# Gated linear attention and SwiGLU: the way down of five blocks by 15 products of 128 columns instead of 7 products of 192

## The chip, the cores and the metric

The kernel runs on one core of a Trainium2 chip. The metric is the device time of one execution in microseconds (us). TensorE (PE) multiplies matrices, VectorE (DVE), ScalarE (ACT) and GpSimd (POOL) work elementwise, SyncE (SP) issues transfers. The instructions of an engine stand in an order that the program fixes, and wait on semaphores for what the other engines have to deliver.

## What is computed

Two stages, all in fp32. The attention runs over 4 batches, 8 heads, 768 positions and 48 features; its output, seen as 3072 tokens of 384 features, is the input of a SwiGLU layer with 1536 hidden features:

```python
f = 1.0 / (1.0 + np.exp(-f_logit))
for t in range(S):
    state = f[:, :, t, :, None] * state + np.einsum('bhd,bhe->bhde', k[:, :, t], v[:, :, t])
    y[:, :, t] = np.einsum('bhd,bhde->bhe', q[:, :, t], state)
x = y.transpose(0, 2, 1, 3).reshape(B * S, H * D)
g = x @ w_gate
return (g * (1.0 / (1.0 + np.exp(-g))) * (x @ w_val)) @ w_out
```

## The kernel before

**Blocks.** The tokens are cut into six blocks, one for each chunk of 128 positions (c = 0 to 5); a block holds 128 positions of 4 batches, 512 tokens. While block c goes through the SwiGLU layer, the attention of chunk c + 1 is worked out between its products. Block 0 is a plain layer (`mlp_plain`: products of 512 columns at L939, then `downs_abreast`: products of 384 columns at L962, whose four results are copied out by ScalarE and VectorE in turn at L983).

**Way up of blocks 1 to 5** (`mlp_fifteen`). Gate and val come from a scheme that multiplies a 3x3 arrangement of weight parts by a 3x2 arrangement of token parts with 15 products in place of 18. The table `PRODUCTS` names for each product r the bank that it is added to (A, B, c or o), the weight part or weight sum, and the token part or token sum (t1 to t15, made by VectorE). There are four such sets of 15 products (`triple(j)`), each product of 256 columns (L1155). Between the products ScalarE copies banks out, VectorE adds, ScalarE applies silu (L1171) and VectorE multiplies by val (L1107); the products of the last two steps finish late (`finish_late`). The hidden activations `h` lie in six parts, by the feature third and the token half.

**Way down of blocks 1 to 5** (`down_seven`). The output of 512 tokens by 384 features is made by a scheme with 7 products in place of 8: each product multiplies one of four parts of `h` (or one of the hidden sums that VectorE makes, 128x768 elements each: `hs` and sums in place of parts of `h`, L1056 and L1059) by half of the columns of `w_out` (or a sum of weights, `ws1`, `ws2`, `ws4`). A product is 12 matmuls of 192 columns by 128 rows; a matmul in fp32 is two instructions, so a block has 168 of them (L1258, the last product L1321). The sums of weights are made once, in block 1, by four multiplications by -1 on ScalarE (L1094) and four accumulating DMAs of 576 KB, which GpSimd's queue issues (L1095).

**What sets the order.** The order is written out by hand. `in_turn_of_time` walks through the products, adds up their planned costs (`PRODUCT`, `DOWN`), and emits a piece of attention when its planned time has come (`SCORES` for the score products, `CHAINS` for the elementwise steps of a chunk and batch, `times`). `lag` puts an operation behind the next product. `in_order` then fixes the order of the instructions on each engine.

**Attention of one batch in a chunk**, as its lines stand: sigmoid by ScalarE (L670, with a table load ahead of it), a transposition on VectorE into `gates` (L681), one of k into `qT` (L692), a running product `tails` (a scan, L702), its reciprocal (L705), `kT` (L648), a transposition for the queue (L722), a second scan (L736), a transposition of q (L740), `qT` (L648), the state (L900) and the decayed state (L654). TensorE uses them in `y` (L836, L847, L872), `dS` (L818) and the scores `sc` (L761, L767), which VectorE masks (L800, L802). The result returns through ScalarE (yT, L854) and ten small DMAs at a time on GpSimd's queue (xT<-yT, L861).

**PSUM.** Banks A (2), B (1), o (2, which c shares) and three for attention.

Of the kernel before, what the change touches and what calls it, by code (L numbers as in the profile page):

```python
# [9 lines left out]
FP32 = mybir.dt.float32  # L10
# [4 lines left out]
ALU = mybir.AluOpType  # L15
# [275 lines left out]
def short_path(ctx, tc, ident, least, judge, q, k, v, f_logit, moe_w_gate, moe_w_val, moe_w_out, out):  # L291
# [633 lines left out]

    def hidden_tile(h, j):


        if j % 2 not in h:
            h[j % 2] = ffn.tile([128, NP // 2, 4, TH], FP32, tag="h", name="h", bufs=2)  # L930
        return h[j % 2][:, j // 2]
# [39 lines left out]
    def downs_abreast(c, h):  # L971
# [3 lines left out]
        def step(n):  # L975
# [3 lines left out]
            for b in range(B):  # L979
                down_part(banks[b], c, h, b, n)  # L980
                if n == NF - 1:
                    ob = rooms_of[b // 2][:, b % 2, :]
                    (nc.vector.tensor_copy if b % 2 else nc.scalar.copy)(ob, banks[b])  # L983
                    nc.gpsimd.dma_start(out=out[b * S + c * C:b * S + (c + 1) * C, :], in_=ob)
# [13 lines left out]
    PRODUCT, DOWN, PLAIN, PLAIN_DOWN = 0.86, 3.9, 2.57, 2.65  # L998
# [10 lines left out]
    whole = NJ * TRIPLE + 7 * DOWN  # L1009
    between = [n * TRIPLE - 0.05 for n in range(NJ)]  # L1010
    inside = [t - PRODUCT for t in between]
    down = [NJ * TRIPLE + n * DOWN / 2 - 0.05 for n in range(14)]
    SCORES = {c: scores for c, scores in zip(range(2, NCH), (
        ((12, "b"), (between[2], "o"), (down[2], "A"), (down[5], "A")),
        ((PRODUCT - 0.05, "b"), (between[1], "o"), (inside[3], "o"), (down[3], "A")),
        *[((down[10] - whole, "A"), (inside[1], "o"), (inside[3], "o"), (down[3], "A"))] * (NCH - 4)))}
    CHAINS = {c: chains for c, chains in zip(range(2, NCH), (
        (chain(2.6, 4.8, 8.6), chain(14.5, 21.7, 23.2, 21.2, 19.6), chain(30, 37, 43.6), chain(57.4, 56.6, 61)),
        (chain(-12, -8.5, -5), chain(3.5, 6, 9), chain(16, 28, 33, 21.5, 23.5), chain(40.1, 53, 55, 44.5, 52)),
        *[(chain(-19.4, -11.2, -9.5), (-7.5, -6.3, 1.3, 2.2, 3.2, 5.5, 8, 10), chain(16, 28, 33, 21.5, 23.5), chain(40.1, 53, 55, 44.5, 52))] * (NCH - 4)))}  # L1020
    LAST = 72.5
    APART = {1: (1, 3), 2: (1, 2), **{c: (2,) for c in range(3, NCH - 1)}, NCH - 1: range(1, NJ)}

    def times(c):
        at = [t for t, _ in SCORES[c]]
        outputs = [*at[1:], down[10] if c + 1 in SCORES and SCORES[c + 1][0][0] < -1 else LAST]
        sigmoid = [-14 if c == 3 else SCORES[c - 1][-1][0] - whole - 0.01 if c > 3 else 0, -1.5 if c == 3 else at[0] - 0.01, *[t - 0.01 for t in at[1:]]]
        masks = {"b": 2, "o": 0.9, "A": 1.5}
# [3 lines left out]
    def score_bank(u):  # L1032
# [4 lines left out]
        return {"o": banks_o, "A": banks_a}[kind].tile([128, 512], FP32, tag=kind, name="sc")  # L1037
# [14 lines left out]
    DOWN_SUMS_AT = (13, 13.01, 26.2, 26.21, 34.5, 34.51, 43, 43.01)  # L1052
# [30 lines left out]
    down_sums = {}  # L1083

    def down_weight_sums():

        DH = DM // 2
        b11, b12 = w_out[:, 0:NP, 0:DH], w_out[:, 0:NP, DH:DM]
        b21, b22 = w_out[:, NP:NF, 0:DH], w_out[:, NP:NF, DH:DM]
        for i in (1, 2, 4):  # L1090
            down_sums[i] = comb.tile([128, NP, DH], FP32, tag=f"ws{i}", name=f"ws{i}")
# [441 lines left out]
```

## Time and profile before

| | |
|---|---|
| median of 3 runs | 589.19 us (588.88 to 590.15) |
| profiled execution | 588.79 us, of which the profile's span is 587.1 us |
| granted TensorE clock | 0.997 |
| PE / DVE / ACT / POOL busy | 576.2 / 472.1 / 306.4 / 116.5 us |
| way down of block 1 | 194.89 to 230.89 us, with attention between its products |
| way down of block 3 | 379.95 to 414.53 us |
| way down of block 5 | from 553.65 us, no attention; last matmul ends at about 582 us |

The profiled execution is 0.4 us below the median; 1.7 us of its time lie outside the span. Times below are microseconds from the start of the span. In a row of the timeline stand the start, the duration from the first start to the last end, the engine, the line, the operation, what it writes and reads, shape and count; consecutive instructions of one kind are one row. A matmul's row contains the time in which its last columns leave the array, so the pace of matmuls is read from the starts of two rows and not from their durations.

### The profile page before, as it was taken

The numbers are of one execution on the slowest core, as the hardware profiler recorded it, in microseconds if no ns is written. First come the engines' busy times: TensorE is split into PE (matmuls) and PEld (weight loads), VectorE is DVE, ScalarE is ACT, GpSimd is POOL, SyncE is SP. The second block draws the span as 40 slices with busy tenths as digits, with TensorE's granted clock in tenths as the row PEclk, the third lists the DMA queues.
The fourth block names the chain that finished last, engine by engine and source line by source line (L and its number), as shares of the span: only waits on it lengthen the run. The fifth ranks groups of instructions, "written<-read, shape, count | busy, mean of one in ns | idle before, by whom it ended". The sixth has DMA issues, their size and how long they took to land.

```text
span 587.1 us, 12325 instructions
## 1 busy us (share of the span) xinstructions
PE 576.2 (98%) x4644; PEld 476.8 (81%) x4644; DVE 472.1 (80%) x828; ACT 306.4 (52%) x589; POOL 116.5 (20%) x253
## 2 busy tenths in 40 slices
PE   7899999999999999999999999999999999999996
PEld 5744445667888999888999888899988899988996
DVE  7978898999989977998985988994978971766641
ACT  2587778023887422677640576732486830366600
POOL 4140344311132241021130030330030330000000
PEclk9999999999999999999999999999999999999998
DMA  9999696433769576462444532444331100100001
GB/s 190 267 284 271 206 231 155 91 106 107 138 145 132 110 164 154 117 118 72 106 107 114 136 88 65 105 110 112 95 101 29 35 13 3 55 1 2 0 1 56
DMA packets 118785, 64.48 MB, mean 110 GB/s; under 512 B 76592, under 2 KB 109168, under 8 KB 118720
## 3 DMA queue, kind: packets, MB, share of 16 engines
q1 hardware_dynamic: 106448, 48.49, 34.0%
q0 software_dynamic: 11120, 13.58, 10.2%
q10 hardware_dynamic: 1152, 1.57, 0.7%
q8 instruction: 37, 0.61, 0.5%
q14 instruction: 28, 0.23, 0.1%
HBM read 49.64 MB, written 8.65 MB: 99 GB/s over the span
## 4 chain that ended last, share of the span: by engine, by line
PE 94%; ACT 2%; DVE 2%; DMA 1%; issue 1%; ACTq 0%; DVEq 0%
PE o L1258 20%; PE A L1155 17%; PE B L1155 14%; PE c L1155 6%; PE o L962 5%; PE o L1155 5%; PE gate L939 5%; PE val L939 5%; PE o L1321 3%; PE y L872 2%; PE dS L818 2%; PE y L836 2%; PE sc L761 2%; PE y L847 2%; DMA fraw<-in_f_logit_dram 1%; PE sc L767 1%
## 5 line engine op out<-in xcount | busy, mean ns | idle before, releaser
L861 POOL DMA_DIRECT2D xT<-yT x120 | 59.7, 506 | 62.6 <-ACT yT L854 57.1
L1258 PE MATMUL o<-w_out,h 128*128 128x192 f32 x360 | 62.0, 327 | 0.0
L1155 PE MATMUL A<-xs,w_both 128*128 128x256 f32 x240 | 61.8, 380 | 0.0
L1258 PEld LDWEIGHTS o<-w_out,h 128*128 128x128 f32 x360 | 58.8, 190 | 0.8 <-issue 0.4
L1160 ACT COPY aside<-A 128x512 f32<-128x512 f32 x60 | 35.1, 586 | 33.1 <-PE A L1155 33.1
L1056 DVE TENSOR_TENSOR c<-c,aside 128x512 f32<-128x512 f32 x60 | 41.2, 687 | 12.5 <-ACT aside L1160 10.8
L1155 PEld LDWEIGHTS A<-xs,w_both 128*128 128x128 f32 x240 | 45.2, 190 | 6.3
L1160 ACT COPY c<-A 128x512 f32<-128x512 f32 x40 | 23.3, 584 | 47.4 <-PE A L1155 39.0
L1107 DVE TENSOR_TENSOR h<-h,c 128x256 f32<-128x256 f32 x100 | 40.5, 413 | 6.2 <-ACT h L1171 5.8
L1059 DVE TENSOR_TENSOR c<-c,aside 128x512 f32<-128x512 f32 x60 | 41.0, 684 | 2.6 <-ACT aside L1160 2.5
L1171 ACT ACTIVATE h<-c 128x256 f32<-128x256 f32 x100 | 39.2, 416 | 4.8 <-DVE c L1056 3.5
L1258 PE MATMUL o<-ws,h 128*128 128x192 f32 x240 | 41.7, 328 | 0.0
L1155 PE MATMUL A<-xs,extra 128*128 128x256 f32 x160 | 41.3, 380 | 0.3 <-ACT c L1160 0.2
L1155 PE MATMUL B<-xs,w_both 128*128 128x256 f32 x160 | 41.3, 380 | 0.0
L1155 PE MATMUL B<-xT,extra 128*128 128x256 f32 x160 | 41.1, 379 | 0.0
L1155 PE MATMUL c<-xT,w_both 128*128 128x256 f32 x160 | 41.0, 379 | 0.0
L1258 PEld LDWEIGHTS o<-ws,h 128*128 128x128 f32 x240 | 39.3, 190 | 0.8 <-issue 0.5
L1160 ACT COPY aside<-B 128x512 f32<-128x512 f32 x60 | 35.1, 585 | 9.0 <-PE B L1155 7.0
L748 POOL MEMSET gates<- 128x4 f32 x24 | 3.6, 150 | 169.9 <-DVE qT L648 159.8
L1059 DVE TENSOR_TENSOR c<-o,c 128x512 f32<-128x512 f32 x40 | 27.4, 685 | 10.4 <-ACT h L1171 5.8
L1056 DVE TENSOR_TENSOR c<-c,o 128x384 f32<-128x384 f32 x15 | 8.2, 550 | 34.2 <-PE o L1258 34.2
L1155 PEld LDWEIGHTS A<-xs,extra 128*128 128x128 f32 x160 | 30.2, 190 | 5.1 <-ACT c L1160 1.1
(176 smaller groups left out, 1256.8 us busy)
## 6 DMA issues: line engine op xcount, KB each, us to landing
fsquares<-in_f_logit_dram SPq DMA_DIRECT2D x64, 96.0 KB, 2.7
qsquares<-in_q_dram SPq DMA_DIRECT2D x64, 96.0 KB, 2.3
ksquares<-in_k_dram SPq DMA_DIRECT2D x64, 96.0 KB, 2.5
w<-in_moe_w_gate_dram SPq DMA_DIRECT2D x6, 768.0 KB, 7.8
w<-in_moe_w_val_dram SPq DMA_DIRECT2D x6, 768.0 KB
w<-in_moe_w_out_dram SPq DMA_DIRECT2D x6, 768.0 KB, 4.6
v<-in_v_dram SPq DMA_DIRECT2D x19, 192.0 KB, 3.1
kt<-turn SPq DMA_DIRECT2D x12, 256.0 KB
```

Of the source, the lines that this page charges most:

```text
L761: nc.tensor.matmul(blocks_of_keys(sc[par], a // 2, a, keys), lhsT=kT[r, a, keys * CH:(keys + 1) * CH], rhs=queries_of_keys(qT[r, a, :], ke ...
L861: (nc.gpsimd if c >= SQUARES else nc.sync).dma_start(out=xT[c][f % 128:f % 128 + n, f // 128, b * C:(b + 1) * C], in_=yT[r:r + n, a // 2, ...
L939: nc.tensor.matmul(p, lhsT=w[:, j, i, :], rhs=xT[c][:, i, :], start=(i == 0), stop=(i == KT - 1))
L962: nc.tensor.matmul(p, lhsT=hidden_tile(h, n // 2)[:, n % 2 * 2 + b // 2, b % 2 * C:(b % 2 + 1) * C], rhs=w_out[:, j, :], start=(n == 0), s ...
L1056: nc.vector.tensor_tensor(dst, a, b, ALU.add)
L1059: nc.vector.tensor_tensor(dst, a, b, ALU.subtract)
L1107: lagging.append(lambda: f(*args))
L1155: nc.tensor.matmul(p[name][:, n, :], lhsT=weights_of[a][:, n, j, :], rhs=tokens[b], start=fresh and n == 0, stop=True, skip_group_check=True)
L1160: nc.scalar.copy(t, p[name])
L1171: nc.scalar.activation(dst, src[:, 0, :], AF.Silu)
L1258: nc.tensor.matmul(p[:, n, :], lhsT=lhsTs[j][:, n * C:(n + 1) * C], rhs=rhs[:, j, :], start=first and j == order[0] and n == 0, stop=j == ...
L1321: nc.tensor.matmul(p, lhsT=hidden_tile(h, j)[:, 2, n * C:(n + 1) * C], rhs=b22[:, j, :], start=j == order[0], stop=j == order[-1])
```

## The change

The way down of blocks 1 to 5 uses the table of 15 products too, with the roles of tokens and weights exchanged: `w_out` is cut into 3x3 parts (four 128x128 pieces each), `h` into its six parts of 128x1024 elements. A product is 8 matmuls of 128 columns by 128 rows (16 instructions), a block has 240 instructions (L1278). One product stands ahead of the last product of the way up, then come r = 5, 8, 11, 0, 1, 3, 4, 6, 7, 9, 10, 12, 13, 14.

- Hidden sums: VectorE makes t1 (in two pieces), t9, t10, t14, t15, t8, t2 and t11, each 128x1024 elements; t5 and t4 are made by a multiplication on ScalarE (L1291) and an accumulating DMA of 512 KB on GpSimd's queue (L1292), t3 by such a DMA alone (L1341).
- Results: ScalarE copies each bank out (`side` or straight into the output), VectorE adds 128x256 elements.
- Weight sums: 11 multiplications on ScalarE (L1106) and 19 accumulating DMAs of 256 KB (L1108) in block 1, in place of 4 and 4.
- `CHAINS`: for the fourth batch of chunks 3 to 5 the second scan, the transposition of q and `qT` are planned up to 4.5 us earlier, inside the last products of the way up.
- Block 0: its four output copies all on ScalarE (L991).
- Last block: its output leaves in column thirds: SP takes columns 128 to 255, GpSimd's queue the upper third, ScalarE's queue the lower third, whose last addition stands on VectorE behind the final ones.

```diff
-                    (nc.vector.tensor_copy if b % 2 else nc.scalar.copy)(ob, banks[b])
+                    nc.scalar.copy(ob, banks[b])
...
-    PRODUCT, DOWN, PLAIN, PLAIN_DOWN = 0.86, 3.9, 2.57, 2.65
+    PRODUCT, DOWN, PLAIN, PLAIN_DOWN = 0.86, 1.75, 2.57, 2.65
...
-        ((12, "b"), (between[2], "o"), (down[2], "A"), (down[5], "A")),
+        ((12, "b"), (between[2], "o"), (down[3], "d"), (down[6], "d")),
...
-        (chain(-12, -8.5, -5), chain(3.5, 6, 9), chain(16, 28, 33, 21.5, 23.5), chain(40.1, 53, 55, 44.5, 52)),
+        (chain(-12, -8.5, -5), chain(3.5, 6, 9), chain(16, 28, 33, 21.5, 23.5), chain(40.1, 49.5, 51, 44.5, 47.5)),
...
+        pieces.insert(-1, (DOWN, downs[2]))
+        return token_sums, pieces + [(0, finish_late)] + [(DOWN, downs[r]) for r in (5, 8, 11, 0, 1, 3, 4, 6, 7, 9, 10, 12, 13, 14)]
...
+            for j in range(NJ):
+                for n in n_of:
+                    nc.tensor.matmul(p[name][:, n, :], lhsT=t[b][:, j, n * C:(n + 1) * C], rhs=a[:, j, :],
...
+        def by_queue(dst, sign, src, added):
+            nc.scalar.mul(dst, src, sign)
+            nc.gpsimd.dma_start(out=dst, in_=added, accum_op=ALU.add)
...
+            if r == 2:
+                late.pop(0)()
+                nc.scalar.copy(part(1, 1), q)
+            elif r == 5:
+                nc.scalar.copy(part(0, 1), q)
+                t["t9"] = kept["xs"][:, NJ:2 * NJ]
+                plus(t["t9"], t["b12"], t["b22"])
+            elif r == 8:
+                nc.scalar.copy(part(2, 0), q)
+                t["t5"] = room("cx2")
+                by_queue(t["t5"], -1.0, t["b11"], t["b32"])
+                t["t10"] = t["b12"]
+                plus(t["t10"], t["b12"], t["b11"])
+                t["t14"] = kept["xs"][:, 0:NJ]
+                minus(t["t14"], t["b21"], t["b31"])
+            elif r == 11:
+                nc.scalar.mul(part(2, 1), q, -1.0)
+                t["t15"] = comb.tile([128, NJ, TH], FP32, tag="hs", name="hs")
+                minus_both(t["t15"], t["b31"], t["b32"])
+                t["t8"] = room("c3x")
+                plus(t["t8"], t["b21"], t["t15"])
+            elif r == 0:
+                nc.scalar.copy(part(0, 0), q)
+                t["t2"] = t["b22"]
+                minus_both(t["t2"], t["t9"], t["t14"])
+                t["t4"] = t["b12"]
+                by_queue(t["t4"], 1.0, t["b11"], t["t9"])
+                t["t3"] = t["b31"]
+                nc.gpsimd.dma_start(out=t["t3"], in_=t["b11"], accum_op=ALU.add)
+            elif r in (1, 6):
+                lag(minus, part(1, 1), part(1, 1), aside(PRODUCTS[r][0]))
...
+            elif r == 13:
+                lag(plus, part(0, 0), part(0, 0), aside("B"))
+                if c == NCH - 1:
+                    for n in range(2):
+                        lag(put_out, 0, n, nc.scalar, slice(0, C))
```

Three places show how the order moves. VectorE's rows in the way down of block 1, before, from the transposition of the gates to `qT`, the last thing that the score product waits for; `h`, `hs` and `A` are hidden sums and masked scores:

```order
L681 STREAM_TRANSPOSE gates_102<-fsquares 128x4x4x32
L692 STREAM_TRANSPOSE qT<-ksquares 128x4x2x2x32
L800 TENSOR_TENSOR A<-sc,diagonals 128x256 x2
L702 SCALAR_TENSOR_TENSOR tails_104<-gates_102,floor 128x516
L705 RECIPROCAL start<-tails_104 128x4
L900 TENSOR_TENSOR state_120<-decayed,dS 128x192
L654 TENSOR_TENSOR decayed<-state_121,least 128x4x48
```

The same place now, where `hs` is t15, `c3x` is t8 and `h<-xs` is t2:

```order
L681 STREAM_TRANSPOSE gates_102<-fsquares 128x4x4x32
L692 STREAM_TRANSPOSE qT<-ksquares 128x4x2x2x32
L1070 SCALAR_TENSOR_TENSOR hs<-h 128x1024
L1064 TENSOR_TENSOR c3x<-h,hs 128x1024
L702 SCALAR_TENSOR_TENSOR tails_104<-gates_102,floor 128x516
L705 RECIPROCAL start<-tails_104 128x4
L800 TENSOR_TENSOR A<-sc,diagonals 128x256 x2
L1070 SCALAR_TENSOR_TENSOR h<-xs 128x1024
L648 TENSOR_TENSOR kT<-qT,tails_104 128x512
L900 TENSOR_TENSOR state_120<-decayed,dS 128x192
L654 TENSOR_TENSOR decayed<-state_121,least 128x4x48
```

Two hidden sums now stand between the transpositions and the scan, and a third, t2, with `kT`, ahead of the decayed state. In both programs L722, the scan L736, L740 and `qT` follow.

ScalarE's rows at the same place before, from the end of the way up to the sigmoid (`c` is the copy of the first down product):

```order
L1171 ACTIVATE h<-A 128x256
L1277 COPY c_1904<-o_1906 128x2x192
L670 ACT_TABLE_LOAD
L670 ACTIVATE fsquares<-fsquares 128x16x32
L854 COPY yT<-y 128x256 x2
```

And now, where the L1315, L1317 and L1321 rows copy products r = 2, 5 and 8, and L1291 is the multiplication for t5:

```order
L1315 COPY ob<-o 128x2x128
L1194 ACTIVATE h<-c_1818 128x256
L1194 ACTIVATE h<-A 128x256
L1317 COPY ob<-o 128x2x128
L1321 COPY ob<-c 128x2x128
L1291 ACTIVATE cx_1944<-h 128x1024
L670 ACT_TABLE_LOAD
L670 ACTIVATE fsquares<-fsquares 128x16x32
```

The table load and the sigmoid have moved behind the copy of the third down product and the multiplication for t5.

VectorE's rows at the end of the way up of block 3, before (with the numbers of the buffers):

```order
L1059 TENSOR_TENSOR c31_3738<-c31_3738,aside_3749 128x512
L1059 TENSOR_TENSOR c32_3731<-c32_3731,c_3735 128x512
L1059 TENSOR_TENSOR c31_3738<-c31_3738,aside_3759 128x512
L1056 TENSOR_TENSOR c11_3671<-c11_3671,aside_3764 128x512
L736 SCALAR_TENSOR_TENSOR gates0_102<-gates0_102,start_106 128x516
L740 STREAM_TRANSPOSE tails0_104<-qsquares_1339 128x4x2x2x32
L1107 TENSOR_TENSOR h_3558<-h_3558,c11_3671 128x256
L1107 TENSOR_TENSOR h_3558<-h_3558,c32_3731 128x256
L1107 TENSOR_TENSOR h_3558<-h_3558,c31_3738 128x256
```

And now, where the two `cx2_3878` rows are t1, which the product r = 5 reads:

```order
L736 SCALAR_TENSOR_TENSOR gates0_102<-gates0_102,start_106 128x516
L1126 TENSOR_TENSOR h_3403<-h_3403,cx2_3797 128x256
L1067 TENSOR_TENSOR c3x_3846<-c3x_3846,aside_3863 128x512
L1067 TENSOR_TENSOR c3x_3846<-c3x_3846,c_3850 128x512
L1064 TENSOR_TENSOR cx2_3878<-h_3403 128x768
L740 STREAM_TRANSPOSE tails0_104<-qsquares_1338 128x4x2x2x32
L1067 TENSOR_TENSOR c3x_3846<-c3x_3846,aside_3875 128x512
L1126 TENSOR_TENSOR h_3403<-h_3403,c3x_3846 128x256
L1064 TENSOR_TENSOR c11_3787<-c11_3787,aside_3888 128x512
L648 TENSOR_TENSOR qT_3803<-tails0_104,gates0_102 128x512
L1064 TENSOR_TENSOR cx2_3878<-h_3403 128x256
```

The scan, the transposition and `qT` have moved ahead of the last multiplications by val, and t1 has come between them.

More of the change, by code (lines that the diff above doesn't have):

```diff
@@ L1176, in one_product @@
                 product(r)
-                if r in FINISH and late:
+                if (r in FINISH or j == order[-1] and r > 12) and late:
                     late.pop(0)()
@@ L1205, in one_product @@
                     finish(2, 1, got[32])
+                    if j == order[-1]:
+                        lag(downs["t1"], 0, NJ - 1)
                 elif r == 12:
@@ L1329, in in_turn_of_time, with first @@
+        downs = {r: (lambda r=r: one(r)) for r in range(len(PRODUCTS))}
+        def first(since, to):
+            if since == 0:
+                names()
+            sum1(since, to)
+        downs["t1"] = first
+        return downs
     def in_turn_of_time(waiting, steps):
@@ L1440, in short_path @@
     waiting += zip(LATE_SUMS_AT, sums[len(SUMS_AT):])
-    waiting += [(at, f) for at, f in zip(DOWN_SUMS_AT, down_weight_sums())]
+    waiting += [(at, f) for at, f in zip(DOWN_SUMS_AT, down_weight_sums(), strict=True)]
     blocks = {}
```

228 lines of the change are left out of this document (114 added, 114 removed).

## Prediction

> **What bounds the kernel now.** I read the page first, for the engine that sets the end, and then the timeline of the stages that the change touches. The page's busy times and its chain of the work that ended last:
>
> ```profile
> PE 576.2 (98%) x4644; PEld 476.8 (81%) x4644; DVE 472.1 (80%) x828; ACT 306.4 (52%) x589; POOL 116.5 (20%) x253
> PE 94%; ACT 2%; DVE 2%; DMA 1%; issue 1%; ACTq 0%; DVEq 0%
> ```
>
> TensorE is the bound: less work for it is time gained, and each wait that the change gives it is time lost. VectorE is at 80% on the average, so the question of every stage is whether its sums come in time.
>
> **The products.** Timeline of TensorE in block 3 (two whole products of 24 instructions) and, far ahead, two groups of four transpositions, each with a 128x128 weight load and 128 columns:
>
> ```profile
> 391.72 4.06 PE L1258 MATMUL o<-w_out,h 128*128 128x192 f32 x24
> 395.62 4.06 PE L1258 MATMUL o<-ws,h 128*128 128x192 f32 x24
> 16.67 0.60 PE L665 MATMUL kTp<-idf,kraw 128*128 128x128 f32 x4
> 17.11 0.60 PE L665 MATMUL qTp<-idf,qraw 128*128 128x128 f32 x4
> ```
>
> From start to start, 192 columns take (395.62 - 391.72) / 24 = 162.5 ns, and 128 columns take 0.44 / 4 = 110 ns. Scaled by columns, 162.5 gives 108 ns. I take 109, with 107 and 114 as the ends. A block's way down now has 168 x 162.5 ns = 27.3 us of products, then 240 x 109 ns = 26.2 us: 1.1 us less, 5.5 us less in five blocks (7.9 less at 107, 0.3 less at 114).
>
> The page "TensorE: Matmul & The Clock Gate" of the Trainium skill speaks against this, in its section on the back-to-back issue gap: in a stream of loads and matmuls, 128 columns come every 81 ns or so where one alone would take 56. By that ratio, an estimate, 109 would become about 158 ns, and a block's products 38 us. The rows of the transpositions, which have a load each, do not show it; they hold no stream longer than some twelve.
>
> **Block 0, copies by ScalarE.** TensorE, VectorE and ScalarE at the end of block 0:
>
> ```profile
> 137.84 1.03 PE L1155 MATMUL B<-xs,w_both 128*128 128x256 f32 x4
> 138.87 0.55 DVE L983 COPY ob<-o 128x384 f32<-128x384 f32 x1
> 139.51 1.10 PE L1155 MATMUL o<-xT,w_both 128*128 128x256 f32 x4 [0.64 <-ACT c L1160]
> 136.53 0.48 ACT L983 COPY ob<-o 128x384 f32<-128x384 f32 x1 [0.81 <-PE o L962]
> ```
>
> The product into bank o could start 0.86 after 137.84, at 138.70. It started at 139.51, just after VectorE's late copy ended at 139.42, which frees the bank (the releaser named is another). ScalarE would do the fourth copy right after the third, by about 137.7. So 0.8 us are gained.
>
> **Block 1, where VectorE gets in the way.** TensorE before, with the first attention group from 198.88 to 201.58 (2.70 us) and the second from 207.63 to 209.72 (2.09 us up to its score product):
>
> ```profile
> 194.89 4.06 PE L1258 MATMUL o<-w_out,h 128*128 128x192 f32 x24
> 198.88 0.45 PE L836 MATMUL y<-qT,decayed 48*32 48x128 f32 x16
> 201.58 4.17 PE L1258 MATMUL o<-ws,h 128*128 128x192 f32 x24
> 207.63 0.45 PE L836 MATMUL y<-qT,decayed 48*32 48x128 f32 x16
> 209.72 1.10 PE L767 MATMUL sc<-qT,kT 48*64 48x128 f32 x32
> ```
>
> Now a product takes 16 x 0.109 = 1.74 us. One stands ahead of the last of the way up, so r = 5 starts at 194.89 + 1.74 = 196.6, r = 8 at 198.4, the group at 200.1, r = 11 at 202.8, r = 0 at 204.5, and r = 1 could start at 206.3.
>
> ScalarE before, and the row from which the multiplication of 1024 elements is read:
>
> ```profile
> 198.99 0.48 ACT L1277 COPY c<-o 128x384 f32<-128x384 f32 x1 [2.25 <-PE o L1258]
> 199.49 1.28 ACT L670 ACT_TABLE_LOAD   x1
> 200.78 0.63 ACT L670 ACTIVATE fsquares<-fsquares 128x512 f32<-128x512 f32 x1
> L1094 ACT ACTIVATE ws<-ws x2: 1163/1165/1167, 169.9 to 187.2; 128x1152 f32<-128x1152 f32 x2
> ```
>
> The copy of r = 8 can end at 200.1 + 0.2 + 0.35 = 200.65. The multiplication for t5 (estimate 1.05 us, from 1.165 for 1152 elements and 0.48 for 384) ends at 201.7, the table load at 203.0, the sigmoid at 203.6. Behind them on ScalarE are queued yT and the copies of the scores.
>
> VectorE before:
>
> ```profile
> 198.22 0.96 DVE L1059 TENSOR_TENSOR h<-h 128x768 f32<-128x768 f32 x1
> 199.09 1.82 DVE L1059 TENSOR_TENSOR h<-hs,h 128x768 f32<-128x768 f32 x2
> 201.50 1.13 DVE L681 STREAM_TRANSPOSE gates<-fsquares 128x512 f32<-128x512 f32 x1 [0.59 <-issue]
> 202.47 0.69 DVE L692 STREAM_TRANSPOSE qT<-ksquares 128x512 f32<-128x512 f32 x1
> 203.06 0.73 DVE L800 TENSOR_TENSOR A<-sc,diagonals 128x256 f32<-128x256 f32 x2
> 203.70 1.23 DVE L702 TENSOR_TENSOR_SCAN tails<-gates,floor 128x516 f32<-128x516 f32 x1
> 205.06 0.33 DVE L900 TENSOR_TENSOR state<-decayed,dS 128x192 f32<-128x192 f32 x1
> 205.70 0.69 DVE L648 TENSOR_TENSOR kT<-qT,tails 128x512 f32<-128x512 f32 x1
> 206.42 0.71 DVE L722 STREAM_TRANSPOSE ksquares<-kT 128x512 f32<-128x512 f32 x1
> 207.05 1.19 DVE L736 TENSOR_TENSOR_SCAN gates<-gates,start 128x516 f32<-128x516 f32 x1
> 208.16 0.68 DVE L740 STREAM_TRANSPOSE tails<-qsquares 128x512 f32<-128x512 f32 x1
> 208.88 0.69 DVE L648 TENSOR_TENSOR qT<-tails,gates 128x512 f32<-128x512 f32 x1
> ```
>
> From start to start, 256 elements take 0.32 us (L800), 512 take 0.59 (L692) and 768 take 0.87 (L1059); each 256 more cost 0.27 to 0.28. So 1024 take an estimated 1.14 us, and 1.22 until the result can be read. No row shows 1024; 0.87 is the nearest below, and nothing shown lets me go under that.
>
> - t9, t10 and t14 end by 201.2, in time for r = 11 and r = 0. Then VectorE waits for the sigmoid until 203.6. L681 and L692 end at 205.2, t15 at 206.3, t8 at 207.5: r = 1 waits **1.2 us** and ends at 209.3.
> - From t8 to the decayed state, which the y group waits for: scan and reciprocal 1.36, masks 0.64, t2 1.14, kT 0.7, states 0.7, together 4.55: 212.05. TensorE waits **2.8 us**.
> - The group lasts to 214.15. VectorE adds transposition 0.63, scan 1.11, transposition 0.7, qT 0.69, and is done at 215.1: the score product waits **0.95 us**, where before it waited some 0.2 (209.72 against the end of the y rows at 209.5).
>
> Together 4.8 us are lost in block 1, against the 1.1 that the products give. The transfers of the weight sums end long before they are read, since their multiplications start 20 us ahead and the pieces are smaller than before.
>
> **Blocks 2, 3 and 4.** VectorE and TensorE at the end of the way up of block 3, and TensorE's attention group in its way down:
>
> ```profile
> 377.33 0.68 DVE L1056 TENSOR_TENSOR c<-c,aside 128x512 f32<-128x512 f32 x1
> 381.38 1.23 DVE L736 TENSOR_TENSOR_SCAN gates<-gates,start 128x516 f32<-128x516 f32 x1
> 379.95 2.11 PE L1258 MATMUL o<-ws,h 128*128 128x192 f32 x12
> 386.76 0.45 PE L836 MATMUL y<-qT,decayed 48*32 48x128 f32 x16
> 389.66 2.22 PE L1258 MATMUL o<-ws,h 128*128 128x192 f32 x12
> ```
>
> Before, the scan ran at 381.38, behind the last sums of the way up. Now it stands directly behind the sum of 377.33, with transposition, qT and t1 also ahead of the product r = 5. The sequence up to the last piece of t1 is 0.61 (sum), 1.14 (scan), 0.33, 0.6, 0.6, 0.87 (t1), 0.61, 0.6, 0.33, 0.6, 0.6 and 0.41 (t1's end): 6.7 us, and 384.0 to 384.6 with the losses between (start 377.33 plus 6.7 to 7.3). TensorE starts r = 2 at 379.95, r = 14 at 381.7, r = 5 at 382.55, and comes to its seventh matmul, the first that reads t1's last piece, at 383.9. I take **0.75 us** of waiting, in each of three blocks: 2.25 us.
>
> Further on, t2 ends 10.65 us after t1 (three short rows, five sums of 1.14, L681, two masks, L692 and t2 itself): 395.25. TensorE reaches r = 3, which reads t2, after r = 5, 8, the group of 2.9 us, r = 11, 0 and 1, at 394.95. **0.3 us** in blocks 2 and 3, 0.6 together. Then t4. GpSimd's queue before, and the landing of the 576 KB sums, minimum, median and maximum:
>
> ```profile
> 389.84 4.46 POOL L861 DMA_DIRECT2D xT<-yT  x9 [4.49 <-ACT yT L854]
> DMA to landing us min/median/max: 6.5/7.0/7.1
> ```
>
> t4's transfer stands behind ten of these (0.5 us each); yT comes at about 391.3, so it is issued at 396.4 and lands, 512 KB for 576, an estimated 6.2 us later, at 402.6. r = 9 reads it at 402.25. I take **0.3 us** for each of the blocks 2 to 4 (0 if it lands in 5 us, 1.2 if it takes 7.1): 0.9.
>
> **Block 5 and the end.** No attention runs there, and I find no wait over 0.1 us. The last rows before:
>
> ```profile
> 582.01 0.35 DVE L1056 TENSOR_TENSOR ob<-c,o 128x192 f32<-128x192 f32 x1 [1.59 <-PE o L1321]
> 582.40 0.35 SPq L1267 DMA_DIRECT2D out_dram<-ob  x1
> ```
>
> Now a further sum of 256 elements follows VectorE's last (0.41) and ScalarE's queue issues two transfers after it (0.35 for the second), less about 0.35 for a shorter last sum and smaller transfers: 0.4 lost.
>
> **Sum**, against the profiled execution of 588.8: -5.5 (products) - 0.8 (block 0) + 4.8 (block 1) + 2.25 + 0.6 + 0.9 (blocks 2 to 4) + 0.4 (end) = +2.65, so 591.45. The median lies 0.4 above the profiled execution: 589.2 + 2.7 = **591.9**.
>
> **Rivals.**
>
> - *Block 1 waits for half as long.* If t8 isn't held up by the sigmoid, because VectorE's chain runs on at 201.2, t8 ends at 205.0, r = 1 doesn't wait, the group waits 1.6 us and the score product 0.95: 2.4 us less, 589.5. For it: ScalarE is 52% busy. Against it: its rows are in order behind r = 8's copy. It decides where the sigmoid ends, 201 or 203.6.
> - *The sums are hidden*, the other side. If VectorE made 1024 elements in under 0.6 us, every wait of blocks 1 to 4 on it would go: 591.9 - 4.8 - 2.85 = 584.2. The three sizes of the L800, L692 and L1059 rows speak against it, a straight line without a faster kind.
> - *Loads set the pace.* If 128 columns can't go below the 162.5 ns that pairs of load and matmul show in the L1258 rows, a block's products take 39 us, 11.7 more than now, 58 in all: 647 instead of 589. The Trainium skill's page named above would have it about there.
> - *t4 late.* If three transfers in a row on a busy queue make t4 land in 9 us, r = 9 waits 3 us in blocks 2 to 4: +8, 600.
>
> **How the numbers follow.** Chances: the forecast 0.52, half the wait 0.2, hidden 0.13, t4 late 0.11, loads 0.04. The forecast's own range is 589 to 594.5 (pace 108 to 111, half a microsecond either way per wait). The range takes in the half wait below and part of t4's case above: 587.0 to 596.0. A measurement of this kernel can tell about 0.2%, 1.2 us, from no change, so same means 588.0 to 590.4. Faster: 0.13 from the hidden case and a part of the second, 0.18. Same: the rest of the half wait and the forecast's lower end, 0.25. Slower: 0.57.
>
> **What would show it.** The L1258 products become L1278 rows of 128 columns at 109 ns; the row after 137.84 starts at 138.7; in block 1 the y rows (L836) of the second group carry an idle time of 2.8 us released by VectorE's L654, the score product one by L648, and r = 1 one by L1064; in blocks 2 to 4 an L1278 row waits 0.75 us for L1064 within r = 5. It is wrong if TensorE runs through block 1 without waiting, or if the products' pace is over 115 ns.

## The result and the profile after

| | before | after |
|---|---|---|
| median of 6 runs | 588.94 us (588.52 to 590.15) | 614.25 us (610.3 to 617.07) |
| ratio to before, 95% interval | | 1.0422 (1.0397 to 1.0447) |
| profiled execution, span | 588.79, 587.1 us | 612.11, 610.3 us |

The change costs some 25 us; the forecast was 2.7, with a range that ended at 596.0. Of e4 and e6 below, one execution each took over 1.5% longer than the fastest of its kernel and is left out of their times; e6's trace is from its one, and is used only for which waits stand in it.

The page of the changed kernel: busy times, granted clock (the share of its full clock that TensorE was given, in tenths, in 40 equal slices), GpSimd's queue of transfers (packets, MB, share of 16 engines; before it read 11120, 13.58, 10.2%) and the chain that ended last.

```profile
PE 581.7 (95%) x5004; PEld 480.9 (79%) x5004; DVE 482.6 (79%) x843; ACT 338.9 (56%) x671; POOL 145.3 (24%) x282
PEclk9999999999999987999999999998999999999998
q0 software_dynamic: 17888, 23.42, 19.3%
PE 77%; DMA 7%; DVE 7%; issue 3%; ACT 3%; SPq 1%; POOL 1%; DVEq 0%; ACTq 0%
```

TensorE's share of the chain fell from 94% to 77%. DMA rose from 1% to 7%, VectorE from 2% to 7%: TensorE now waits. From block 1 on, its waits of 0.4 us and more add up to 7.7 us for transfers, 5.1 for VectorE and 3.4 for ScalarE. Where the 23.2 us of the span went: a way up is counted from its first matmul's start to the way down's first, a way down from there to its last matmul's start (the new order counts 0.86 us of block 1's way up to its way down).

| us | block 1 | block 2 | block 3 | block 4 | block 5 |
|---|---|---|---|---|---|
| way up before, after | 57.9, 60.1 | 57.8, 57.8 | 56.7, 56.7 | 55.5, 55.5 | 51.1, 51.1 |
| way down before, after | 35.8, 48.3 | 34.4, 36.3 | 34.4, 39.3 | 32.4, 32.8 | 28.0, 28.3 |

Block 1 holds 14.7 us of it, blocks 2 and 3 hold 6.7, blocks 4 and 5 0.7, and 1.3 lie behind the last product; the steps from block to block give 0.2 back. TensorE's rows after, with the idle time ahead of a row in brackets: the first products of block 1, the third of which used to wait for block 0's last copy (three rows), then the waits of block 1, the waits for t1 and for t4, and block 4.

```profile
136.97 1.03 PE L1173 MATMUL A<-xs,w_both 128*128 128x256 f32 x4
137.83 1.03 PE L1173 MATMUL B<-xs,w_both 128*128 128x256 f32 x4
138.69 1.03 PE L1173 MATMUL o<-xT,w_both 128*128 128x256 f32 x4
...
155.27 1.13 PE L1173 MATMUL A<-xs,w_both 128*128 128x256 f32 x4 [1.57 <-ACT c L1183]
185.76 1.13 PE L1173 MATMUL B<-xs,w_both 128*128 128x256 f32 x4 [0.60 <-ACT aside L1183]
211.02 2.02 PE L1278 MATMUL B<-w_out,c3x 128*128 128x128 f32 x16 [1.08 <-DVE c3x L1064]
215.36 0.45 PE L836 MATMUL y<-qT,decayed 48*32 48x128 f32 x16 [2.31 <-DVE decayed L654]
234.76 1.10 PE L818 MATMUL dS<-v,kt 128*64 128x48 f32 x16 [3.42 <-DMA kt<-turn]
235.79 3.78 PE L1278 MATMUL B<-w_out,hs 128*128 128x128 f32 x16
239.37 2.74 PE L1278 MATMUL A<-w_out,c3x 128*128 128x128 f32 x16
241.94 1.95 PE L1278 MATMUL B<-ws,h 128*128 128x128 f32 x16
...
307.99 0.71 PE L1278 MATMUL o<-ws,cx 128*128 128x128 f32 x4 [0.57 <-DVE cx L1064]
327.36 1.91 PE L1278 MATMUL A<-ws,h 128*128 128x128 f32 x15 [1.22 <-DMA h<-xs]
421.83 3.65 PE L1278 MATMUL A<-ws,h 128*128 128x128 f32 x16 [2.55 <-DMA h<-xs]
425.41 0.86 PE L872 MATMUL y<-qT,diagonal 128*32 128x128 f32 x24
...
509.77 1.95 PE L1278 MATMUL A<-ws,xs 128*128 128x128 f32 x16
511.56 1.95 PE L1278 MATMUL B<-ws,cx 128*128 128x128 f32 x16
```

Several kinds of loss stand here. The waits released by VectorE are the forecast ones: r = 1 (1.08), the y group (2.31), t1 (0.57). The waits for transfers, `kt` (3.42) and t4 (1.22 and 2.55), are not, but for the 0.3 us that each block's t4 was given; nor are those for ScalarE's copies in the way up (1.57 and 0.60). And behind a long wait the same product takes twice its time: 239.37 - 235.79 = 3.58 us for 16 instructions that take 511.56 - 509.77 = 1.79 in block 4, and again 425.41 - 421.83 = 3.58 behind the wait for t4. The windows of the profile give the granted clock there, in the column after the five engines (then the DMA share and GB/s):

```profile
235.80:240.80 5.00, 5.00 (x25) 5.00 (x24) 0.79 (x2) 0.37 (x1) 0.62 (x2) 0.50 0.80 204
241.00:245.00 4.00, 4.00 (x38) 4.00 (x37) 2.65 (x8) 0.74 (x2) 0.10 (x1) 1.00 0.71 167
421.90:425.40 3.50, 3.50 (x16) 3.30 (x16) 1.11 (x1) 0.00 (x0) 0.00 (x0) 0.51 0.55 119
428.60:432.00 3.40, 3.40 (x31) 3.40 (x32) 1.70 (x5) 0.81 (x3) 0.00 (x0) 1.00 0.54 154
```

The clock is half for some microseconds behind these waits and then whole again. The trace's record of the clock has three such stretches before the end: 217.12 to 220.53 us (behind the wait of the y group and one of 0.53 us after it), 234.18 to 241.01 (`kt`) and 421.92 to 425.33 (t4 in block 3). A long wait is thus paid twice in part: products at half the clock lose half of the stretch, an estimated 1.7, 3.1 and 1.7 us, 6.5 together (the second stretch begins in the wait itself, 0.58 us before its end).

GpSimd's queue of block 1 shows what two of the waits in the way up hang on: transfers of weight sums that wait for each other's landing (the first below landed at 168.81, the second at 173.59), and a clearing of `gates` (L748) behind them.

```profile
163.65 1.28 POOL L1108 DMA_DIRECT2D w_out<-w_out  x1 [4.37 <-ACT least L733]
169.09 1.27 POOL L1108 DMA_DIRECT2D w_out<-w_out  x1 [4.17 <-DMA w_out<-w_out]
174.10 1.27 POOL L1108 DMA_DIRECT2D w_out<-ws  x1 [3.74 <-issue]
174.85 0.63 POOL L748 MEMSET gates<- 128x4 f32 x1
```

VectorE's next row, which writes into the cleared `gates`:

```profile
175.52 1.19 DVE L681 STREAM_TRANSPOSE gates<-fsquares 128x512 f32<-128x512 f32 x1 [2.58 <-POOL gates L748]
```

VectorE lost 2.58 us there, behind the clearing of four columns that stood in line behind three transfers, and TensorE lost 0.79 and 0.60 soon after (at 179.19 and 185.76).

### The profile page after: what moved, and what is told of

The parts are those of the page before. It is cut to its first block, busy times and chain, and to the rows that moved or that the text cites. A ratio compares the mean times of both kernels' runs of the same rounds, so it can differ in the third digit from the quotient of the medians.

```text
span 610.3 us, 13265 instructions
## 1 busy us (share of the span) xinstructions
PE 581.7 (95%) x5004; PEld 480.9 (79%) x5004; DVE 482.6 (79%) x843; ACT 338.9 (56%) x671; POOL 145.3 (24%) x282
## 4 chain that ended last, share of the span: by engine, by line
PE 77%; DMA 7%; DVE 7%; issue 3%; ACT 3%; SPq 1%; POOL 1%; DVEq 0%; ACTq 0%
PE A L1173 14%; PE B L1173 12%; PE A L1278 7%; PE B L1278 6%; PE o L970 5%; PE gate L947 5%; PE val L947 5%; PE o L1173 5%; PE c L1173 4%; DMA h<-xs 3%; DMA kt<-turn 2%; PE c L1278 2%; PE y L872 2%; PE dS L818 2%; PE sc L761 2%
## 5 line engine op out<-in xcount | busy, mean ns | idle before, releaser
L748 POOL MEMSET gates<- 128x4 f32 x24 | 4.1, 172 | 146.4 <-DVE qT L648 141.3
L1067 DVE TENSOR_TENSOR cx<-o,cx 128x512 f32<-128x512 f32 x40 | 27.4, 685 | 12.6 <-ACT h L1194 6.9
L1173 PEld LDWEIGHTS B<-xs,w_both 128*128 128x128 f32 x160 | 30.2, 190 | 6.2 <-ACT c3x L1183 1.2
L1067 DVE TENSOR_TENSOR ob<-ob,side 128x256 f32<-128x256 f32 x29 | 12.0, 419 | 28.6 <-ACT side L1287 28.6
L1173 PEld LDWEIGHTS B<-xT,extra 128*128 128x128 f32 x160 | 30.3, 190 | 4.4 <-ACT aside L1183 0.3
L1173 PEld LDWEIGHTS c<-xT,w_both 128*128 128x128 f32 x160 | 30.4, 190 | 4.1
L947 PE MATMUL gate<-xT,w_both 128*128 128x512 f32 x72 | 32.3, 595 | 0.0
L970 PE MATMUL o<-w_out,h 128*128 128x384 f32 x96 | 32.2, 490 | 0.0
L947 PE MATMUL val<-xT,w_both 128*128 128x512 f32 x72 | 32.1, 594 | 0.0
L702 DVE TENSOR_TENSOR_SCAN tails<-gates,floor 128x516 f32<-128x516 f32 (+1 forms) x25 | 29.4, 1177 | 1.5 <-ACT gates L677 1.5
L1287 ACT COPY side<-B 128x256 f32<-128x256 f32 x25 | 9.3, 372 | 37.7 <-PE B L1278 33.8
L736 DVE TENSOR_TENSOR_SCAN gates<-gates,start 128x516 f32<-128x516 f32 x24 | 29.2, 1216 | 0.0
```

What stands on the lines that cost most here:

```text
L702: nc.vector.tensor_tensor_scan(tail[:, at][:, ::-1], gate[:, at][:, ::-1], floor[:, at][:, ::-1], 1.0, op0=ALU.mult, op1=ALU.max)
L736: nc.vector.tensor_tensor_scan(gate[:, 0:n], gate[:, 0:n], start, 1.0, op0=ALU.mult, op1=ALU.add)
L947: nc.tensor.matmul(p, lhsT=w[:, j, i, :], rhs=xT[c][:, i, :], start=(i == 0), stop=(i == KT - 1))
L970: nc.tensor.matmul(p, lhsT=hidden_tile(h, n // 2)[:, n % 2 * 2 + b // 2, b % 2 * C:(b % 2 + 1) * C], rhs=w_out[:, j, :], start=(n == 0), s ...
L1067: nc.vector.tensor_tensor(dst, a, b, ALU.subtract)
L1173: nc.tensor.matmul(p[name][:, n, :], lhsT=weights_of[a][:, n, j, :], rhs=tokens[b], start=fresh and n == 0, stop=True, skip_group_check=True)
```

## Experiments

**Which transfers cost how much.** My theory after the result: the added accumulating transfers cost most, by their own waits and by what they do to other transfers. The rival: VectorE's longer sums in block 1, as the prediction had it, cost more than I counted. Three kernels leave transfers out, and nothing else; the sums then lack their second parts.

Without the transfers of the weight sums (e3). The trace has 16 of them (L1108) and 10 multiplications (L1106); the 19 and 11 of "The change", and the 19 of the expectations, are miscounted.

```diff
-            for a in added:
-                nc.gpsimd.dma_start(out=dst, in_=a, accum_op=ALU.add)
```

> The changed kernel without the 19 accumulating transfers of the weight sums (the products then use sums that lack their second part). Queue and bandwidth theories alike: block 1's way up loses its waits (4 us), and its way down is spared the late transfer of k if that came from them: 606 to 610. VectorE theory, that the time went to the hidden sums in VectorE's order: 613 to 614.

Without the transfers of t5, t4 and t3 (e4):

```diff
-            nc.gpsimd.dma_start(out=dst, in_=added, accum_op=ALU.add)
...
-                nc.gpsimd.dma_start(out=t["t3"], in_=t["b11"], accum_op=ALU.add)
```

> The changed kernel without the transfers that complete t5, t4 and t3 in each block (these sums then lack their second part). Queue theory: the waits for t4 in blocks 2 and 3 go (1.2 and 2.6 us, and the slower clock behind the second), and the late transfer of k in block 1 (3.4 us, and the slower clock behind it): 602 to 607. VectorE theory: 613.

Without either, by both edits (e5):

> The changed kernel without both kinds of transfers: those of the weight sums and those that complete t5, t4 and t3 (the sums lack their second parts). What is left is the prediction's own ledger. By it: 591.9 forecast, less 0.9 for t4, plus 3.2 for a pace of 111.7 and not 109 ns: 594. If the two kinds of transfers cost independently, 614.3 - 9.3 - 12.8 = 592. Rival, that one kind only hides the other: 599 to 601.

| | before | after | e3, no weight sums | e4, no t5, t4, t3 | e5, neither |
|---|---|---|---|---|---|
| median us | 588.94 | 614.25 | 604.98 (603.49 to 606.61) | 599.96 (598.46 to 602.88) | 596.9 (594.51 to 599.98) |
| ratio to before, 95% | | 1.0422 | 1.0257 (1.0213 to 1.03) | 1.0157 (1.0106 to 1.0207) | 1.0134 (1.0075 to 1.0193) |
| block 1 up, down | 57.9, 35.8 | 60.1, 48.3 | 55.6, 44.5 | 61.5, 43.1 | 55.6, 41.7 |
| block 2, block 3 down | 34.4, 34.4 | 36.3, 39.3 | 36.4, 37.1 | 34.8, 34.8 | 34.8, 34.8 |
| longest wait for `kt` | none | 3.42 | 1.16 | 0.35 | 0.71 |
| waits for t4 | | 1.22, 2.55 | 1.28, 2.03 | none | none |
| waits for t8, decayed state | none | 1.08, 2.31 | 1.08, 2.32 | 1.08, 2.32 | 1.08, 2.32 |
| DMA share, 135 to 250 us | 0.65 | 0.82 | 0.52 | 0.74 | 0.46 |

All three are still over the kernel before. The transfers carry 614.25 - 596.9 = 17.4 of the 25 us. By the medians, leaving out one kind saves 9.3 or 14.3, more than 17.4 together, as if the two kinds hindered each other. The traces don't bear this out: block 1, up and down, takes 108.4 us after, 100.1 in e3, 104.6 in e4 and 97.3 in e5, so that the weight sums cost 8.3 us there beside the transfers of t5, t4 and t3, and 7.3 without them. VectorE's waits are the same in all four kernels (last row but one), so the rival can't explain the 17.4; the half clock that follows the wait of 2.3 us in three of the traces comes on top (see the clock below). Without transfers the prediction's list is nearly right (point by point below). TensorE's waits in block 1 of e5:

```profile
207.35 2.02 PE L1276 MATMUL B<-w_out,c3x 128*128 128x128 f32 x16 [1.08 <-DVE c3x L1064]
211.69 0.45 PE L836 MATMUL y<-qT,decayed 48*32 48x128 f32 x16 [2.32 <-DVE decayed L654]
212.57 0.67 PE L818 MATMUL dS<-v,kt 128*64 128x48 f32 x16 [0.43 <-DMA kt<-turn]
214.75 1.10 PE L767 MATMUL sc<-qT,kT 48*64 48x128 f32 x32 [0.46 <-DVE qT L648]
227.38 0.67 PE L818 MATMUL dS<-v,kt 128*64 128x48 f32 x16 [0.71 <-DMA kt<-turn]
```

How an added transfer reaches TensorE is seen on SP's queue, which issues the attention's own. In the changed kernel, the four transfers that turn the squares of k, and `kt` behind them:

```profile
215.95 5.24 SPq L725 DMA_DIRECT2D turn<-ksquares  x4
223.06 1.76 SPq L497 DMA_DIRECT2D ksquares<-in_k_dram  x4
224.88 2.38 SPq L497 DMA_DIRECT2D qsquares<-in_q_dram  x4
227.35 0.57 SPq L789 DMA_DIRECT2D kt<-turn  x1
```

The same in e5:

```profile
212.28 3.41 SPq L725 DMA_DIRECT2D turn<-ksquares  x4
215.94 1.86 SPq L497 DMA_DIRECT2D ksquares<-in_k_dram  x4
217.86 1.85 SPq L497 DMA_DIRECT2D qsquares<-in_q_dram  x4
219.81 0.57 SPq L789 DMA_DIRECT2D kt<-turn  x1
```

The turning takes 5.24 us to issue in place of 3.41 (2.63 in the kernel before), beside the transfers of t4 and t3 that GpSimd's queue issued at 212.4 and 213.0. From the start of the turning to `kt` it is 11.4 us in place of 7.5. `kt` itself takes as long in both until TensorE goes on, 7.4 and 7.6 us (227.35 to 234.76, 219.81 to 227.38): it is late because it was issued late. The turning takes 4.97 us in e3 and 3.79 in e4, and from its start to `kt` it is 10.95 and 8.06: t4's and t3's transfers make `kt` late, with the weight sums or without them. That e3 waits only 1.16 for it fits its clock, which is half from 215.75 to 222.57 us there and keeps TensorE itself back.

**Contention or the wait for the sums?** If the sums came earlier, would they be free? This kernel clears `gates` on VectorE (next experiment) and issues every transfer of the weight sums at its place and size, but into pieces that no product reads.

```diff
-        down_parts.update({f"e{n}": t for n, t in enumerate(e)})
+        down_parts.update({f"e{n}": w[n // 2, n % 2] for n in range(6)})
...
-            ..., (a13, -1.0, a33, a21, a31, e[3]),
+            ..., (e[4], -1.0, a33, a21, a31, e[3]),
```

> This is the changed kernel with the clearing of `gates` on VectorE, as in the run that cleared it there (612.2 us), and with one thing more: all 19 transfers of the weight sums are issued at the same places and with the same sizes, but they only add into the six spare pieces, and the products read pieces of the loaded weights, so that no product waits for a sum. Left out: the right weights in the products on the way down, so the output is not the reference's. Theory A (contention: what costs is that these transfers run, and delay the attention's own transfers of `A` to `turn` and to `kt` and of `yT`): the waits of the first block up (ScalarE's copies behind `turn`, 2.6 us) and for `kt` (3 to 5 us) stay, only the 3.0 us for the weights of r=11 and the half clock behind it (1.7 us) go; 607 to 609 us. Theory B (what costs is the wait for the sums themselves, so that earlier or better ordered sums could have been free): the time falls to that of the kernel without the sums, 605 us, and the landing of the transfers of `A` to `turn` has no part in it. The waits for `h` of 1 and 2 us in the two middle blocks stay in both.

609.64 us (607.25 to 614.36), ratio 1.0337 (1.0318 to 1.0357), which is 608.0 to 610.3 us: at the upper end of theory A, with B's 605 outside. Its waits for `kt` and for ScalarE's copies in the way up (2.61) stayed; the wait of r = 11 for a sum went.

```profile
238.84 0.67 PE L818 MATMUL dS<-v,kt 128*64 128x48 f32 x16 [4.31 <-DMA kt<-turn]
```

By the rows of block 1, up and down, e13 takes 106.8 us, the kernel that reads the same sums (e2, below) 107.8, and e3, without them, 100.1. Median landing of the four transfers of `A` to `turn` between 135 and 250 us, first e13:

```profile
turn<-A SPq DMA_DIRECT2D x4, 64.0 KB, 6.1
```

and e5:

```profile
turn<-A SPq DMA_DIRECT2D x4, 64.0 KB, 2.2
```

It is 6.5 in the changed kernel, 5.8 in e4 and 2.2 before. So these transfers cost by running, whether a product waits for them or not. ScalarE's copy of the scores into `A` (L772) writes where these four transfers read. It stood waiting for 4.29 us in the changed kernel, 5.19 in e13 and 0.04 in e5, with the bank copies of the way up in line behind it; that the landing released it is inferred, the profile doesn't name it.

**The clearing behind the transfers** (e2): L748 on VectorE.

```diff
-        nc.gpsimd.memset(pairs(gate)[:, :, 0:1], 0.0)
+        nc.vector.memset(pairs(gate)[:, :, 0:1], 0.0)
```

> The changed kernel, with the small clearing of the gates (128x4 elements) on VectorE and not on GpSimd. Queue theory: in block 1 the clearing stood on GpSimd behind weight sums that wait for the landing of others, VectorE waited 2.6 us for it and TensorE some 3 us soon after; that goes, 611 against 614. Bandwidth theory: the transfers themselves are slow, the order on GpSimd does not matter: 614.

612.18 us (610.99 to 618.1), ratio 1.0399 (1.0341 to 1.0457): overlapping the changed kernel's interval, so no gain that can be told. The 0.79 and 0.60 went (way up 58.8 in place of 60.1), and another came, for a weight sum itself:

```profile
209.68 2.70 PE L1278 MATMUL c<-w_out,h 128*128 128x128 f32 x16 [3.04 <-DMA w_out<-w_out]
236.46 1.10 PE L818 MATMUL dS<-v,kt 128*64 128x48 f32 x16 [5.36 <-DMA kt<-turn]
```

**Other orders of the sums.** e9 is e2 with the sum that r = 11 reads made ahead of two others; e11 is e9 with the first sums started later, and so closer together:

```diff
-            (a11, ...), (e[3], ...), (a21, -1.0, a21, a22), (a22, 0, None, a23, a32), (a31, -1.0, a31, a32))]
+            (a11, ...), (e[3], ...), (a31, -1.0, a31, a32), (a21, -1.0, a21, a22), (a22, 0, None, a23, a32))]
...
-    DOWN_SUMS_AT = (0.5, 2.4, 4.4, 6.4, 9, 9.01, 15, 21, 27, 30, 36, 39.4, 45.4)
+    DOWN_SUMS_AT = (13, 14.5, 16, 17.5, 19, 19.01, 21, 25, 29, 31, 36, 39.4, 45.4)
```

> The changed kernel with the gates cleared by VectorE, and with one weight sum (a31, which r = 11 reads) made ahead of the two that wait for each other. Queue theory: with the clearing alone, r = 11 came to wait 3.0 us for that sum, and the clock fell behind the wait (1.7 us); both go, 612 - 4.7 = 607.5. Rival, transfers too slow in any order: the wait moves to the late transfer of k or to t5, and the time stays near 612.

> As e9_sumorder, with the first weight sums planned 12 us later, so that they no longer run beside the transposing transfer of k at 145 to 152 us. If the transfers get in each other's way there, the wait of 2.6 us for ScalarE's copy at 158 goes and the time is 2 to 3 us under e9_sumorder. Rival: the same number of transfers in less time makes the later ones late, and nothing is won or up to 3 us lost.

615.12 us, ratio 1.0445 (1.0379 to 1.0511), and 621.44, ratio 1.0525 (1.0466 to 1.0585): the first no better than the changed kernel, the second worse. In e9 the first down product now waits 1.06 for a sum, and the way up 3.60 for ScalarE. In e11 the wait in the way up fell to 0.35 there and came back as 3.74 at 177.7 and, for a sum, at 208.2:

```profile
208.17 3.75 PE L1278 MATMUL o<-w_out,h 128*128 128x128 f32 x16 [4.13 <-DMA w_out<-w_out]
```

No order that I tried gets the sums past the attention's transfers for less.

**t4 and VectorE's order.** e6 is the changed kernel with t4 made by VectorE, without multiplication and transfer:

```diff
-                by_queue(t["t4"], 1.0, t["b11"], t["t9"])
+                plus(t["t4"], t["b11"], t["t9"])
```

> The changed kernel, all sums whole, with t4 made by VectorE (one more sum of 128x1024) and not by ScalarE and GpSimd's queue. Queue theory: the waits of the product r = 9 for t4 in blocks 2 and 3 go, with the slow clock behind the second: 614 - 1.2 - 2.6 - 1.9 = 608, and VectorE's 1.14 us more per block cost under 1. VectorE theory: the sum only moves the wait to t11 or to the scan behind it: 613 or more.

606.43 us (602.71 to 609.38), ratio 1.0274 (1.021 to 1.0338). The waits for `h<-xs` are gone, and a ScalarE copy (`side`, L1287) is waited for in their place. The wait for `kt` is gone too, though t3's transfer is still there, which points at t4's. By the medians t4's transfer was worth 7.8 of the 14.3 us that e4 won.

e7 is e5 with the third score product of chunk 2 planned two products later, so that the y group does not wait for VectorE:

```diff
-        ((12, "b"), (between[2], "o"), (down[3], "d"), (down[6], "d")),
+        ((12, "b"), (between[2], "o"), (down[3], "d"), (down[8], "d")),
```

> As the kernel without both kinds of transfers, with the y group and the score product of the third batch in block 1 planned two products later, behind r = 4. VectorE theory: the wait of 2.3 us for the decayed state goes, and nothing else of block 1's down does: 3 us under the kernel without both. Rival, that the group's followers (masks, next gates) are late in their turn: the same time.

595.26 us (594.95 to 599.08), ratio 1.0111 (1.006 to 1.0161), beside e5's 1.0134: the same. The wait of 2.32 went. In its place r = 3 waits 1.15 for t2 and a later y group 2.53 for ScalarE's `diagonal` (L660).

e8 is e5 with the old `CHAINS` for the fourth batch, so that the scan no longer stands ahead of t1:

```diff
-... chain(40.1, 49.5, 51, 44.5, 47.5)
+... chain(40.1, 53, 55, 44.5, 52)
```

> As the kernel without both kinds of transfers, with the times of the fourth batch's scan, transposition and qT put back to those of before. Theory of the prediction: the wait for t1 (0.57 us in blocks 2, 3 and 4) goes, since 1.2 us of rows no longer stand ahead of its last piece: 1.7 us under the kernel without both. Rival: the score product, which waits for qT, or t10, which moves behind it, waits instead, and the time stays or grows.

595.6 us (593.76 to 597.06), ratio 1.0092 (1.0063 to 1.0122), overlapping e5's. The waits for t1 went in three blocks, r = 3 waits 0.61 for t2 in blocks 2 and 3 instead, and block 4's way down is 0.8 us shorter (31.92 for 32.75).

e12 takes e11, t4 by VectorE, the later score product and the old `CHAINS` together:

> As e11_spread, with everything else that helped alone: t4 by VectorE, the second y group in block 1 two products later, the fourth batch's scan at its old time. If the waits add up, 597 to 601, still over the kernel before; if VectorE's further sum takes back what the others give, 603 to 606. Under 589 only if the products themselves gain, which their measured pace of 111.7 ns does not give.

615.2 us (615.05 to 615.8), ratio 1.0436 (1.0418 to 1.0453). Block 2 and 3 came down to 36.1, block 1 did not (66.1 up and 48.6 down). The same y group now waits longer:

```profile
240.47 1.66 PE L872 MATMUL y<-qT,diagonal 128*32 128x128 f32 x21 [4.63 <-ACT diagonal L660]
```

**The copies of block 0 alone** (e1): the kernel before, with this line of the change.

```diff
-                    (nc.vector.tensor_copy if b % 2 else nc.scalar.copy)(ob, banks[b])
+                    nc.scalar.copy(ob, banks[b])
```

> The kernel before with one line of the change: the four output copies of block 0 all on ScalarE. If the late copy on VectorE is what held the product at 139.51, TensorE gains 0.8 us and nothing gives it back: 588.1 against 588.9. Rival: the start of block 1 is held by something else soon after, and the time stays 588.9.

588.11 us (587.7 to 591.67) beside 589.67, ratio 0.9976 (0.9956 to 0.9996), a gain of a quarter of a percent. It is the only version here that beats the kernel before.

## Why the prediction was wrong

The direction was right and the size was not: 2.7 us more forecast, 25 measured. **The step that failed** is the sentence "The transfers of the weight sums end long before they are read, since their multiplications start 20 us ahead and the pieces are smaller than before". It costed the transfers at nothing by asking only when their data are read. They cost 9.3 us by the medians (after less e3), 8.3 by the rows of block 1, for the most part by running: they fill the DMA engines (a share of 0.82 in block 1 for 0.65 before), slow the attention's transfers (6.5 us for 2.2 from `A` to `turn`), and hold GpSimd's queue at each other's landings with the clearing of `gates` in line. Where no product reads the sums, block 1 is still 6.7 us longer than without their transfers, of 7.7 where the products do (e13 and e2 against e3). My "smaller pieces" were also more of them: 16 x 256 KB are 4.2 MB, 4 x 576 KB were 2.4. Nor did they end long ahead: the last landed at 205.19 us, and r = 11, which reads it, began at 206.11.

**t4's landing** was the second step, right in mechanism and wrong in size: "lands, 512 KB for 576, an estimated 6.2 us later", 0.3 us in each of three blocks. Leaving out the transfers of t5, t4 and t3 won 14.3 us by the medians, for the 0.9 in the sum. Three windows of the changed kernel around these transfers, blocks 2, 3 and 4 (the DMA share is the last column but one):

```profile
314.00:328.00 14.00, 12.78 (x115) 12.61 (x114) 12.67 (x21) 5.20 (x14) 6.91 (x13) 1.00 0.89 184
405.00:422.00 17.00, 14.45 (x177) 14.11 (x170) 13.73 (x22) 7.32 (x16) 7.83 (x14) 1.00 0.86 178
495.00:512.00 17.00, 16.45 (x213) 15.77 (x212) 11.60 (x18) 7.21 (x17) 7.81 (x14) 1.00 0.34 67
```

and the landing of t4's transfer in each:

```profile
h<-xs POOLq DMA_DIRECT2D x1, 512.0 KB, 7.1
...
h<-xs POOLq DMA_DIRECT2D x1, 512.0 KB, 9.3
...
h<-xs POOLq DMA_DIRECT2D x1, 512.0 KB, 4.6
```

The same transfer takes 7.1 and 9.3 us where loads for the next chunk fill the engines, and 4.6 in block 4, where there are few. I had taken a landing from another stage and given it to all blocks; the row that I took it from also holds three of the four sums only, and the fourth, into `w_out`, landed in 8.4 us. The rival "t4 late" named the mechanism (9 us, 3 us in each of three blocks); it came true in block 3 (2.55), half in block 2 (1.22), not in block 4. These transfers also made `kt` late, which no part of the prediction had (3.42 us, 0.35 in e4).

**The clock behind the waits** was in no term: an estimated 6.5 us in the changed kernel, as worked out above. Whether a wait is followed by half the clock can be read off the traces. The stretches begin on a fixed grid: in the changed kernel the three starts lie 17.06 and 187.74 us apart, which is 5 and 55 steps of 3.413 us, and each lasts one step or two. I added up TensorE's idle time in each step of all fourteen traces. From block 1 on, of the steps that had the whole clock, all 25 with 2.03 us or more of idle time are followed by half the clock, and none of the others, which had at most 1.97; in block 0 three are, with 2.08, 1.98 and 1.54, in three traces. So the same wait of 2.32 us is followed by half the clock in e4, where it lies within one step (up to 218.72 us), and not in e5, where a step ends at 211.33 us inside it and leaves 1.96 us in the one and 0.36 in the next. Windows behind it, first e4, then e5:

```profile
218.40:221.00 2.60, 2.25 (x48) 1.89 (x52) 2.56 (x4) 0.00 (x0) 0.00 (x0) 0.56 0.34 60
```

```profile
212.00:217.00 5.00, 4.11 (x110) 3.60 (x99) 4.11 (x7) 0.68 (x2) 1.77 (x5) 1.00 0.44 75
```

e5's four executions took 594.51 and 594.52 us at mean granted clocks of 0.998 and 1.000, and 599.27 and 599.98 at 0.991 and 0.990. The same waits falling elsewhere on the grid would explain that, but only the first of the four was traced. Differences of a few microseconds between these kernels therefore say little without their rows.

The section on the HAM clock gate of the Trainium skill's page "TensorE: Matmul & The Clock Gate" says that the clock falls to half after an idle window of some 3.4 us. The steps of 3.41 us agree with that; but a step need not be idle throughout, 2.03 us of it were enough here.

The other points:

- *Products at 109 ns, 5.5 us gained.* 1.787 us per 16 instructions are 111.7 ns, inside the ends of 107 and 114: 26.8 for 27.3 us a block, 2.5 us in five blocks. The 3 us less are most of the gap between e5's span (5.7 us over before) and the sum without t4's 0.9, +1.75. The rival "Loads set the pace" is not seen: 128 columns take well under 162.5 ns.
- *Block 0, 0.8.* Right: the third row starts at 138.69, forecast 138.7, and e1 shortens the way up of block 1 by 0.9 us.
- *Block 1's waits, 1.2, 2.8, 0.95.* 1.08, 2.31 and 0.46 (e5): right in place and order, the last at half its size. The sum of 1024 elements took the estimated 1.14 us from start to start.
- *t1, 0.75 in three blocks.* 0.57, 0.56 and 0.55. (The steps listed up to t1's end add up to 7.3 us, not 6.7; the 0.75 follows from 7.3.) *t2, 0.3.* Nothing until t1's wait is taken away (e8), then 0.61.
- *The end, 0.4.* 1.3 us, with 0.1 in e5. The last issue ends 4.75 us before the span's end, for 4.3 before and 3.5 in e5; why, stays open.
- *Block 5, no wait over 0.1.* One of 0.46 us, for a bank that ScalarE copies (582.15).

What stays open besides: whether the two kinds of transfers make each other dearer, where medians and rows disagree; and how much of the changed kernel's 25 us another placement of its waits on the clock's grid would give back.

## What to carry to other kernels

A transfer that nobody waits for is not free: look at the DMA share of the stage that it is put into and at the landing of the transfers that stand there already, and price the delay of those. What stands behind it on the same queue, down to a clearing of four columns, waits with it. A wait of some two microseconds or more on TensorE cost up to three more in clock here, so price it for more than its length. A scheme that saves one multiplication in 21 has half a microsecond a block to spend, and one wait for a sum takes that.

## What the runs showed of the hardware

- A pair of weight load and product of 128 columns in fp32 comes every 111.7 ns in a stream of 240, where 192 columns took 162.5: the time goes with the columns (162.5 scaled is 108.3), with some 3% lost at the smaller size.
- Issuing four transfers of 64 KB on SP's queue took 2.63 us in the kernel before, 3.41 in e5 and 5.24 in the changed kernel, beside two accumulating transfers of 512 KB.
- The accumulating transfer of 512 KB for t4 landed in 4.6 us in block 4, at a DMA share of 0.34, and in 7.1 and 9.3 in blocks 2 and 3, at 0.89 and 0.86.
- TensorE's granted clock changed on a grid of 3.41 us. From block 1 on it was half, for 3.41 or 6.83 us, behind each step at the whole clock in which TensorE idled 2.03 us or more, and behind none with 1.97 or less.
